# Scores of batches 4 to 7 on 64-partition heads, the first attention-values step ahead of the second scores, and the values prepared a batch ahead

## The chip, the cores and the metric

The kernel runs on one core of one Trainium2 chip. The metric is device time in microseconds (us), lower is better. The kernel before takes 320.43 us as the median of three runs (319.01 to 321.49); the profiled execution took 320.42 us, of which the span between its first and last instruction is 318.6 us.

## The reference

Two things in a row: an attention over q, k, v of shape (8 batches, 8 heads, 576 positions, 64), and a feed-forward layer over its output seen as 4608 rows of 512 columns.

```python
q_d, k_d, v_d = means of q, k, v over 4 neighbouring positions      # 144 positions
out_d = softmax(q_d @ k_d.T / 8) @ v_d                              # each row repeated 4 times
scores = where(|i - j| < 4, q @ k.T / 8, -1e9)                      # a band of 7
out   = repeat(out_d, 4) + softmax(scores) @ v
x     = out as 4608 x 512                                           # row: batch and position
h     = x @ w_in                                                    # 512 -> 2048
g     = h * sigmoid(1.702 * h)
y     = g @ w_out                                                   # 2048 -> 512
```

## The kernel before

The order of instructions on every engine is written out by hand: each engine runs its own in the order in which the program issues them, and semaphores join the engines.

**Groups.** After a prologue that does batch 0's attention, the main loop runs over nine groups `g` of 512 rows. Group `g` does the feed-forward layer of its rows: `mm1` (16 chunks of 128 hidden columns, four matmuls of 128x512 each, L712, each chunk followed by an activation `silu` on ScalarE, L723), then `mm2` (64 matmuls of 128x512, L776; after each 16 of them an output tile is scaled on ScalarE and stored from SyncE's queue). Beside that, group `g` does the attention of batch `b = g + 1`, as steps put between these matmuls. The list `POS` says where: its numbers count mm1's chunks from 0 to 15, and from 16 on mm2's matmuls (position n is matmul n - 16). The steps are, in order:

1. `s_pe(0)` at 13: the scores of heads 0 to 3 on TensorE. `scores_mixed` takes three PSUM tiles: two for the band (5 stretches of 60 queries against 64 keys, two halves `par`, four heads `r`, and two halves `a` of the head dimension: 80 matmuls of 32 rows, L360) and one for the coarse scores (24 matmuls of 32 rows and 144 columns, L372).
2. `s_act(0)` at 16: a table load, two exponentials of the band (`es`, L410) and one of the coarse scores (`ed`, L416) on ScalarE; the band mask on VectorE (`mask_local`, L424).
3. `s1` at 35: scores and exponentials of heads 4 to 7.
4. `avn(0, 1)` at 45: for head pairs 0 and 1 the products with the values, 40 matmuls each (L441 with `vb`, L463 with the coarse values `vd`), then `normalise` on VectorE (reciprocal L479, multiply L480).
5. `av_tr` at 56: the same for pairs 2 and 3, and the transposes of pair 0.
6. `tr(1, 2, 3)` at 69: the other transposes (L494, L504), copies on ScalarE (L618) and the merges into `xT` on VectorE (L639, L645). `xT` is what the next group's mm1 reads.

Three PSUM tiles `PA` of two banks go round in turn for all of these steps, two banks `PM` for the feed-forward layer.

**q and k.** A load by GpSimd's queue (`load_1`, L185) brings four heads of one batch as bf16 into 128 partitions. `prep_1` (L262) transposes 32x32 blocks on VectorE, so that head `r` lies on partitions 32r to 32r + 31, each holding pairs of head dimensions next to each other (`a`). `pool_qk` (L292, L296) sums over four positions on GpSimd, for `kdT` and `qdT`. The load buffers are double (`bufs=2`).

**Values.** SyncE's queue loads v in fp32 for the band (`vf`, ten transfers, L205, one buffer) and for the coarse sums (`v4`, six transfers, L228, one buffer). In group g GpSimd casts batch b's `vf` to `vb` (`prep_v`, L302) and sums `v4` into `vd` (`prep_v4`, L308 and L311, three times). `vbs` and `vds` are double, by the parity of the batch.

**Preparation in a group.** Before the steps, each group from 1 on issues this:

```python
if b > 2: load_v4(b)
prep_qk(b, 0); pool_qk(b, 0)
if b + 1 < B: load_qk(b + 1, 0 and 1)
prep_v(b, nc.gpsimd)
if b + 1 < B: load_v(b + 1)
prep_qk(b, 1); pool_qk(b, 1)
prep_v4(b, nc.gpsimd)
```

Of the kernel before, what the change touches and what calls it, by code (L numbers as in the profile page):

```python
# [8 lines left out]
FP32 = mybir.dt.float32  # L9
# [10 lines left out]
def kernel(  # L20
# [43 lines left out]
    eds = [persist.tile([128, 2, 480], BF16, name=f"ed{i}") for i in range(2)]  # L64
    v4 = persist.tile([128, 3, HP, 4 * D], FP32, name="v4")
    kdT = [persist.tile([128, 160, 2], BF16, name=f"kdT{i}") for i in range(NQ)]

    PA = [psum.tile([128, 2, 512], FP32, name=f"pa{i}") for i in range(3)]
    PM = [psum.tile([128, 512], FP32, name=f"pm{i}") for i in range(2)]
# [2 lines left out]
    def ps_tile(n=None):  # L72
        if n is None:
            n = turn["a"] % 3
            turn["a"] += 1
        return PA[n]
# [3 lines left out]
        return PM[turn["m"] % 2]  # L80

    wz = consts.tile([128, 512], BF16, name="wz")
    wf = consts.tile([128, 512], FP32, name="wf")
    off = consts.tile([128, 60], BF16, name="off")
    psel = consts.tile([128, 7, 64], BF16, name="psel")

# [24 lines left out]
    def fill():  # L111
        nc.vector.memset(wz, 0.0)
        nc.vector.memset(wf, 0.0)
        for t in kdT:
            nc.vector.memset(t[:, SD:160, :], 0.0)
        for t in vbs:
            nc.vector.memset(t[:, :, :, 64:65], 1.0)
        for t in vds:
            nc.vector.memset(t[:, :, :, 64:65], 4.0)
        for t in es:  # L120
            nc.vector.memset(t[:, :, 300:304], 1.0)
        for t in eds:
            nc.vector.memset(t[:, :, 432:480], 1.0)
# [56 lines left out]

    def load_1(name, src, store, b, qd):
        t = ldp.tile(
            [128, 1152], BF16, name=f"{name}b{qd}", tag=f"{name}b{qd}", bufs=2
        )
        nc.gpsimd.dma_start(  # L185
            out=t,
            in_=bass.AP(
                tensor=src.tensor, offset=src[b, 4 * qd].offset,
                ap=[[1152, 128], [1, 1152]],
            ),  # L190
        )
        store[b, qd] = t

    def load_qk(b, qd):
        load_1("k", k, kf, b, qd)
        load_1("q", q, qf, b, qd)
# [61 lines left out]
    def prep_1(name, b, qd):  # L258
        store, dst = {"k": (kf, kT), "q": (qf, qT)}[name]
        tt = work.tile([128, S, 2], BF16, name=f"{name}T{qd}", tag=f"{name}T{qd}", bufs=1)  # L260
        t32 = tt.rearrange("p t a -> p (t a)").bitcast(FP32)
        nc.vector.transpose(  # L262
            out=t32.rearrange("p (i c) -> p c i", c=18),
            in_=store[b, qd].bitcast(FP32).rearrange("p (c d) -> p c d", c=18),
        )
        dst[b, qd] = tt

    def prep_qk(b, qd):
        prep_1("k", b, qd)
        prep_1("q", b, qd)  # L270

    def new_qdT(b, qd):
        t = work.tile([128, SD, 2], BF16, name=f"qdT{qd}", tag=f"qdT{qd}", bufs=1)
# [115 lines left out]
    def scores_d(b, qd, sd):  # L389
# [3 lines left out]
                    score_d(b, qd, sd, kc, a, r)  # L393
        return sd

    def scores_mixed(b, qd):
        sp, sd = [ps_tile(), ps_tile()], ps_tile()
        for i in range(5):
            for a in range(2):
                if i >= 2:  # L400
                    for r in range(4):
                        score_d(b, qd, sd, i - 2, a, r)
                for x in (1, 0):
                    for r in range(4):
                        score(b, qd, sp, i, a, r % 2 if x == 0 else 1 - r % 2, r)
        return sp, sd
# [254 lines left out]
    def attention(b, slots=None):  # L661
        st = {}

        def s_pe(qd):
            st["s", qd], st["d", qd] = scores_mixed(b, qd)

        def s_act(qd):
            if qd == 0:
                nc.scalar.preload_act_table_set("exp_and_others")
            exp_local(qd, st["s", qd])  # L670
            exp_down(qd, st["d", qd])
            if qd == 1:
                nc.scalar.preload_act_table_set("silu_and_others")
            mask_local(qd)

        def s1():
            s_pe(1)
            s_act(1)

        def avn(*hps):  # L680
            def f():
                for hp in hps:
                    st["o", hp] = av(b, hp, slots and slots[hp % 2])
                for hp in hps:
                    st["y", hp] = normalise(st["o", hp])
            return f

        def tr(*hps):
            def f():
                for hp in hps:  # L690
                    st["x", hp] = transp(st["y", hp], slots and slots[hp % 2])
                for hp in hps:
                    od = copy_od(st["x", hp])
                    merge(b, hp, st["x", hp], od)
            return f

        first = [lambda: s_pe(0), lambda: s_act(0), s1, avn(0, 1)]
        if b == 1:
            return first + [tr(0), tr(1), avn(2, 3), tr(2), tr(3)]

        def av_tr():
            for hp in (2, 3):
                st["o", hp] = av(b, hp)
            st["x", 0] = transp(st["y", 0])
            for hp in (2, 3):
                st["y", hp] = normalise(st["o", hp])
            merge(b, 0, st["x", 0], copy_od(st["x", 0]))

        return first + [av_tr, tr(1, 2, 3)]

    def hps_mm(g, ffc, dmc, acc):
# [91 lines left out]
            f()  # L803

    POS = [13, 16, 35, 45, 56, 69]
    POS_0 = [16, 18, 30, 46, 52, 56, 65, 71, 75]
    VDP_0 = 41

# [93 lines left out]
    for g in range(n_groups):  # L902
        b = g + 1
        if g == 0:
            load_vb(1, 0)
            load_vb(1, 1)
            load_vb(1, 2)
            prep_qk(1, 0)
            pool_qk(1, 0)
            prep_qk(1, 1)  # L910
            load_vb(1, 3)
            load_vb(1, 4)
            load_w_out(2)
            load_w_out(3)
            reduce_qk(1, 1, "q")
            reduce_qk(1, 1, "k")
            for qd in range(NQ):
                load_qk(2, qd)
            nc.gpsimd.memset(v4[32:64], 0.0)
            load_v(2, gate=after(w_out_bf[0:1, 12, 0:1], nc.gpsimd))  # L920
            load_v4(2)
        elif b < B:
            if b > 2:
                load_v4(b)
            prep_qk(b, 0)
            pool_qk(b, 0)
            if b + 1 < B:
                for qd in range(NQ):
                    load_qk(b + 1, qd)
            prep_v(b, nc.gpsimd)  # L930
            if b + 1 < B:
                load_v(b + 1)
            prep_qk(b, 1)
            pool_qk(b, 1)
            prep_v4(b, nc.gpsimd)
        steps = {}
        if b < B:
            for n, f in zip(POS if g else POS_0, attention(b, None if g else (1, 2))):
                steps.setdefault(n, []).append(f)
            if g == 0:  # L940
                steps.setdefault(VDP_0, []).append(lambda: prep_vd_pe(1, flat(PA[2])))
        gT = new_gT() if g else gT0
        mm1(g, gT, steps, 0 if g else 6)
        mm2(g, gT, {n - 16: f for n, f in steps.items() if n >= 16})
# [30 lines left out]
```

## Time and profile before

| what | value |
|---|---|
| median of 3 runs | 320.43 us (319.01 to 321.49) |
| profiled execution: time, span | 320.42 us, 318.6 us |
| busy share of the span: TensorE, VectorE, ScalarE, GpSimd | 97%, 42%, 58%, 44% |
| granted TensorE clock in the 40 slices | 9 (90% or more) throughout |
| groups 3 to 6 (batches 4 to 7): length of each | 32.86, 32.99, 33.09, 32.75 us |
| group 7 (no attention): length | 27.63 us |

Times in the profile are in us from the first instruction unless marked ns. PE is TensorE's matmuls, PEld its weight loads, DVE VectorE, ACT ScalarE, POOL GpSimd, SP SyncE. A line "x32" in a timeline is 32 instructions merged, with the first one's start and the time from there to the last one's end. A 128x512 matmul is listed with 380 ns, but the next one starts 0.216 us later, so the stream is read from starts.

### The profile page before, as it was taken

Reading aid. Unit: us, or ns where it says so; the run is one execution under the profiler, and the core shown is the slowest. Engines: PE = TensorE matmul, PEld = TensorE weight load, DVE = VectorE, ACT = ScalarE, POOL = GpSimd, SP = SyncE. Lnnn points to the kernel's source line nnn. Section 1 sums busy time; section 2 is a strip of 40 time slices with the busy share of each in tenths; the row PEclk is TensorE's granted clock in tenths of the full one; section 3 lists DMA queues with packets and bytes.
Section 4 is the critical chain, followed back from the end, with each engine's and each line's share of the span. In section 5 each row is a group of like instructions: output and inputs, shape, how many; then the busy total and the mean of one; then the engine's idle time right before and its main releaser. Section 6 shows DMA issues by size and latency. Waiting matters only on the chain.

```text
span 318.6 us, 10993 instructions
## 1 busy us (share of the span) xinstructions
PE 309.5 (97%) x4927; PEld 156.9 (49%) x4927; DVE 133.6 (42%) x222; ACT 184.0 (58%) x314; POOL 138.9 (44%) x168
## 2 busy tenths in 40 slices
PE   7899999999999989999999999999999999999995
PEld 4465455444554545455545554455445544444444
DVE  6963825730684066703780378027811650000000
ACT  4464773577647674658465846674667556415611
POOL 8843782099209930696049703980297000000000
PEclk9999999999999999999999999999999999999999
DMA  7999999999719941598259915991360110020011
GB/s 121 116 191 209 184 90 207 185 270 230 180 39 218 199 114 70 144 216 173 71 134 206 188 41 136 206 205 58 109 107 2 71 68 2 0 99 33 2 65 67
DMA packets 64078, 40.02 MB, mean 126 GB/s; under 512 B 44064, under 2 KB 55456, under 8 KB 64032
## 3 DMA queue, kind: packets, MB, share of 16 engines
q0 software_dynamic: 19392, 14.95, 33.3%
q1 hardware_dynamic: 44496, 24.32, 32.7%
q8 instruction: 38, 0.62, 0.9%
q10 hardware_dynamic: 144, 0.07, 0.1%
q14 instruction: 8, 0.07, 0.1%
HBM read 44.83 MB, written 9.44 MB: 170 GB/s over the span
## 4 chain that ended last, share of the span: by engine, by line
PE 86%; DMA 7%; POOL 4%; issue 1%; ACT 0%; DVE 0%; POOLq 0%
PE pm L776 37%; PE pm L712 33%; DMA kb<-in_k_dram 5%; PE pa L360 3%; PE pa L776 2%; DMA qb<-in_q_dram 2%; PE pa L441 2%; PE pa L712 2%; PE pa L494 2%; PE pa L372 2%; PE pa L463 2%; PE pm L791 1%; POOL w_in_bf L238 1%; POOL vb L216 1%; POOL pq L292 1%
## 5 line engine op out<-in xcount | busy, mean ns | idle before, releaser
L776 PE MATMUL pm<-w_out_bf,gT 128*128 128x512 bf16 x528 | 120.8, 380 | 0.4 <-issue 0.4
L712 PE MATMUL pm<-xT,w_in_bf 128*128 128x512 bf16 x512 | 119.2, 379 | 0.0
L723 ACT ACTIVATE gT<-pm 128x512 bf16<-128x512 f32 x128 | 76.3, 598 | 44.7 <-PE pm L712 44.7
L712 PEld LDWEIGHTS <-w_in_bf 128*128 128x128 bf16 x576 | 55.6, 98 | 66.2
L776 PEld LDWEIGHTS <-gT 128*128 128x128 bf16 x560 | 52.0, 98 | 60.8 <-issue 1.7
L424 DVE TENSOR_TENSOR es<-es,mask 128x600 bf16<-128x600 bf16 x28 | 18.6, 667 | 90.1 <-ACT es L410 89.1
L292 POOL TENSOR_TENSOR pq<-kT 128x576 f32<-128x576 bf16 x13 | 15.1, 1159 | 84.7 <-DVE kT L262 84.7
L761 ACT ACTIVATE osb<-pm 128x512 f32<-128x512 f32 (+2 forms) x35 | 20.5, 586 | 38.3 <-PE pm L776 34.2
L618 ACT COPY od<-pa 128x384 f32<-128x384 f32 (+1 forms) x56 | 19.0, 406 | 26.4 <-PE pa L504 23.3
L480 DVE TENSOR_TENSOR y<-pa,rc 128x896 bf16<-128x896 f32 x28 | 30.6, 1092 | 1.0
L410 ACT ACTIVATE es<-pa 128x600 bf16<-128x600 f32 x32 | 19.7, 668 | 10.8 <-PE pa L360 10.6
L639 DVE TENSOR_TENSOR xT<-pa,od 128x570 bf16<-128x570 f32 x28 | 21.0, 752 | 8.0 <-ACT od L618 8.0
L308 POOL TENSOR_TENSOR v<-v 112x512 f32<-112x512 f32 x18 | 23.9, 1330 | 0.0
L763 DVE TENSOR_SCALAR osb<-pm 128x128 f32<-128x128 f32 x1 | 0.3, 293 | 55.0 <-ACT osb L761 55.0
L262 DVE STREAM_TRANSPOSE kT<-kb 128x576 f32<-128x576 f32 x16 | 20.0, 1248 | 5.6 <-DMA kb<-in_k_dram 5.5
L262 DVE STREAM_TRANSPOSE qT<-qb 128x576 f32<-128x576 f32 x16 | 19.8, 1240 | 0.8 <-DMA qb<-in_q_dram 0.6
L712 PE MATMUL pa<-xT,w_in_bf 128*128 128x512 bf16 x64 | 20.0, 379 | 0.0
L360 PEld LDWEIGHTS <-kT 32*64 32x64 bf16 x1280 | 14.7, 104 | 7.8 <-issue 6.6
L360 PE MATMUL pa<-qT,kT 32*64 32x60 bf16 x1280 | 17.2, 198 | 1.3 <-DVE qT L262 1.3
L216 POOL DMA_DIRECT2D vb<-in_v_dram x20 | 13.7, 699 | 8.1 <-DMA w_in_bf<-in_moe_w_in_dram 3.6
L292 POOL TENSOR_TENSOR pq<-qT 128x576 f32<-128x576 bf16 x13 | 14.9, 1147 | 0.0
L416 ACT ACTIVATE ed<-pa 128x864 bf16<-128x864 f32 x16 | 14.3, 897 | 0.1
(92 smaller groups left out, 278.9 us busy)
## 6 DMA issues: line engine op xcount, KB each, us to landing
out_dram<-osb SPq DMA_DIRECT2D x35, 256.0 KB, 2.1
vf<-in_v_dram SPq DMA_DIRECT2D x60, 128.0 KB, 5.3
v<-in_v_dram SPq DMA_DIRECT2D x36, 192.0 KB, 4.5
kb<-in_k_dram POOLq DMA_DIRECT2D x16, 288.0 KB, 6.5
qb<-in_q_dram POOLq DMA_DIRECT2D x16, 288.0 KB, 7.9
w_in_bf<-in_moe_w_in_dram POOLq DMA_DIRECT2D x4, 512.0 KB, 12.1
w_out_bf<-in_moe_w_out_dram POOLq DMA_DIRECT2D x4, 512.0 KB, 8.7
vb<-in_v_dram POOLq DMA_DIRECT2D x20, 64.0 KB, 5.7
```

The costliest lines, as they stand in the source:

```text
L262: nc.vector.transpose(out=t32.rearrange("p (i c) -> p c i", c=18), in_=store[b, qd].bitcast(FP32).rearrange("p (c d) -> p c d", c=18),)
L292: nc.gpsimd.tensor_tensor(out=t1, in0=sv[:, :, 0:2, :], in1=sv[:, :, 2:4, :], op=ALU.add)
L308: eng.tensor_tensor(out=t1[0:112], in0=x[:, :, 0:2, :], in1=x[:, :, 2:4, :], op=ALU.add)
L360: nc.tensor.matmul(sp[r // 2][64 * par : 64 * par + 64, r % 2, 60 * i : 60 * i + 60], lhsT=kT[b, qd][rows, k0 : k0 + 64, a], rhs=qT[b, qd] ...
L410: nc.scalar.activation(out=es[2 * qd + u][:, :, 0:300], in_=sp[u][:, :, 0:300], func=AF.Exp, scale=inv_sqrt_d,)
L480: nc.vector.tensor_tensor(out=y[:, xs], in0=ov[:, :, :, 0:D], in1=rc[:, xs].to_broadcast([128, n, 7, D]), op=ALU.mult,)
L618: nc.scalar.copy(out=od[:, 4 * t0 : 4 * (t0 + n)].rearrange("p (t f) -> p t f", f=4), in_=x[:, xx, 288 : 288 + n, None].to_broadcast([128, ...
L639: eng.tensor_tensor(out=sub(xT[hp], t0 + 3, (57, 2), (114, 5), (1, 57)), in0=sub(x, 3, (509, 2), (57, 5), (1, 57)), in1=sub(od, 3, (57, 2) ...
L712: nc.tensor.matmul(acc, lhsT=w_in_bf[:, dmc, ffc * 128 : (ffc + 1) * 128], rhs=xT[dmc][:, g * TG : g * TG + TG], start=(dmc == 0), stop=(d ...
L723: nc.scalar.activation(out=gT[:, ffc, :], in_=acc, func=AF.Silu, scale=GELU_SCALE)
L761: eng.activation(out=osb, in_=ap, func=AF.Copy, scale=1.0 / GELU_SCALE)
L776: nc.tensor.matmul(ops[t], lhsT=gT[:, ffc, t * 128 : (t + 1) * 128], rhs=w_out_bf[:, ffc, :], start=(ffc == 0), stop=(ffc == n_ffc - 1),)
```

## The change

For batches 4 to 7 (`WIDE = 4`, groups 3 to 6):

- After the transpose of q or k, `widen` makes a copy with a head on 64 partitions: one VectorE copy of 128 partitions x 1152 elements that separates the two halves `a`, and four copies of 32 partitions x 576 that gather each head's halves above each other. Two heads lie on the partitions at a time, the other two (`x`) behind them. `pool_wide` sums these on GpSimd as `pool_qk` did.
- `scores_wide` takes 40 matmuls of 64 rows for the band and 12 for the coarse scores, in place of 80 and 24 of 32 rows.
- The order of preparation on VectorE is: transpose k0, widen k0, transpose q0, transpose k1, widen q0, transpose q1, widen k1, widen q1. Each load for the next batch is issued behind its transpose.
- `avn(0, 1)` goes ahead of `s1`; the steps stand at `POS_W` = 14, 16, 35, 46, 59, 71.
- `vb` and `vd` of the next batch are prepared on GpSimd at the end of a group's preparation, from loads that SyncE issues at the group's start.

In all batches the load buffers of q and k are single. `wf` lies in `v4`'s memory. In groups 1 and 2 the preparation changes over: in group 1 VectorE casts `vf` and sums `v4` for batch 2, GpSimd casts batch 3's `vf`, and `v4` of batch 3 is loaded at position 70; in group 2 VectorE sums `v4` for batch 3, and GpSimd casts and sums for batch 4.

```diff
@@ persistent tiles
+    kdW = [persist.tile([128, 2, 160], BF16, name=f"kdW{i}") for i in range(NQ)]
+    qdW = [persist.tile([128, 2, SD], BF16, name=f"qdW{i}") for i in range(NQ)]
+    kW = [persist.tile([128, 2, S], BF16, name=f"kW{i}") for i in range(NQ)]
+    qW = [persist.tile([128, 2, S], BF16, name=f"qW{i}") for i in range(NQ)]
+    WIDE = 4
-    wf = consts.tile([128, 512], FP32, name="wf")
+    wf = v4.rearrange("p k h c -> p (k h c)")[:, 0:512]
@@ fill()
+        for t in kdW:
+            nc.vector.memset(t[:, :, SD:160], 0.0)
@@ load_1()
-            [128, 1152], BF16, name=f"{name}b{qd}", tag=f"{name}b{qd}", bufs=2
+            [128, 1152], BF16, name=f"{name}b{qd}", tag=f"{name}b{qd}", bufs=1
@@ new functions
+    def widen(name, b, qd):
+        src = (kT if name == "k" else qT)[b, qd]
+        w = (kW if name == "k" else qW)[qd]
+        nc.vector.tensor_copy(out=w, in_=src.rearrange("p t a -> p a t"))
+        for s in range(2):
+            lo, hi = slice(64 * s, 64 * s + 32), slice(64 * s + 32, 64 * s + 64)
+            nc.vector.tensor_copy(out=w[hi, 0, :], in_=w[lo, 1, :])
+            nc.vector.tensor_copy(out=w[lo, 1, :], in_=src[hi, :, 0])
+
+    def pool_wide(name, qd):
+        src, dst = (kW[qd], kdW[qd][:, :, 0:SD]) if name == "k" else (qW[qd], qdW[qd])
+        sv = src.rearrange("p x (j f) -> p (x j) f", f=4)
+        t1 = work.tile([128, 2, SD, 2], FP32, name="pq", tag="pq")
+        nc.gpsimd.tensor_tensor(
+            out=t1.rearrange("p x j f -> p (x j) f"),
+            in0=sv[:, :, 0:2], in1=sv[:, :, 2:4], op=ALU.add,
+        )
+        nc.gpsimd.tensor_tensor(
+            out=dst, in0=t1[:, :, :, 0], in1=t1[:, :, :, 1], op=ALU.add
+        )
+
+    def prep_wide(b):
+        def turn_load(name, qd):
+            prep_1(name, b, qd)
+            if b + 1 < B:
+                load_1(name, *((k, kf) if name == "k" else (q, qf)), b + 1, qd)
+        def finish(name, qd):
+            widen(name, b, qd)
+            pool_wide(name, qd)
+        turn_load("k", 0)
+        finish("k", 0)
+        turn_load("q", 0)
+        turn_load("k", 1)
+        finish("q", 0)
+        turn_load("q", 1)
+        finish("k", 1)
+        finish("q", 1)
+
+    def scores_wide(qd):
+        sp, sd = [ps_tile(), ps_tile()], ps_tile()
+        for i in range(5):
+            for x in range(2):
+                for s in range(2):
+                    rows = slice(64 * s, 64 * s + 64)
+                    for par in range(2):
+                        k0 = 114 * i + KSTART[par]
+                        q0 = 114 * i + QSTART[par]
+                        nc.tensor.matmul(
+                            sp[s][64 * par : 64 * par + 64, x, 60 * i : 60 * i + 60],
+                            lhsT=kW[qd][rows, x, k0 : k0 + 64],
+                            rhs=qW[qd][rows, x, q0 : q0 + 60],
+                            start=True, stop=True,
+                            tile_position=(64 * s, 64 * par),
+                        )
+            if 1 <= i < 4:
+                kc = i - 1
+                for s in range(2):
+                    rows = slice(64 * s, 64 * s + 64)
+                    for x in range(2):
+                        nc.tensor.matmul(
+                            sd[64 * x : 64 * x + 64, s, SD * kc : SD * kc + SD],
+                            lhsT=kdW[qd][rows, x, 48 * kc : 48 * kc + 64],
+                            rhs=qdW[qd][rows, x, :],
+                            start=True, stop=True,
+                            tile_position=(64 * s, 64 * x),
+                        )
+        return sp, sd
@@ scores_mixed()
+        if b >= WIDE:
+            return scores_wide(qd)
@@ attention()
+        if b >= WIDE:
+            first = first[:2] + [avn(0, 1), s1]
@@ main loop
     POS = [13, 16, 35, 45, 56, 69]
+    POS_W = [14, 16, 35, 46, 59, 71]
...
-        elif b < B:
-            if b > 2:
-                load_v4(b)
+        elif b < WIDE:
+            if b == WIDE - 1:
+                load_v(b + 1)
             prep_qk(b, 0)
             pool_qk(b, 0)
-            if b + 1 < B:
-                for qd in range(NQ):
-                    load_qk(b + 1, qd)
-            prep_v(b, nc.gpsimd)
+            prep_qk(b, 1)
+            for qd in range(NQ):
+                load_qk(b + 1, qd)
+            if b < WIDE - 1:
+                prep_v(b, nc.vector)
+                load_v(b + 1)
+            prep_v4(b, nc.vector)
+            pool_qk(b, 1)
+            prep_v(b + 1, nc.gpsimd)
+            if b == WIDE - 1:
+                load_v4(b + 1)
+                prep_v4(b + 1, nc.gpsimd)
+        elif b < B:
             if b + 1 < B:
                 load_v(b + 1)
-            prep_qk(b, 1)
-            pool_qk(b, 1)
-            prep_v4(b, nc.gpsimd)
+                load_v4(b + 1)
+            prep_wide(b)
+            if b + 1 < B:
+                prep_v(b + 1, nc.gpsimd)
+                prep_v4(b + 1, nc.gpsimd)
         steps = {}
         if b < B:
-            for n, f in zip(POS if g else POS_0, attention(b, None if g else (1, 2))):
+            for n, f in zip(POS_W if b >= WIDE else POS if g else POS_0, attention(b, None if g else (1, 2))):
                 steps.setdefault(n, []).append(f)
+            if b == WIDE - 2:
+                steps.setdefault(70, []).append(lambda: load_v4(WIDE - 1))
```

## The prediction

> **What bounds the kernel now.** I read the page first (busy shares, chain that ended last), then the windows view over groups 3 to 7, then timelines of single groups. TensorE is busy 97% of the span and makes 86% of the chain; no other engine reaches 60%.
>
> ```profile
> PE 309.5 (97%) x4927; PEld 156.9 (49%) x4927; DVE 133.6 (42%) x222; ACT 184.0 (58%) x314; POOL 138.9 (44%) x168
> ...
> PE 86%; DMA 7%; POOL 4%; issue 1%; ACT 0%; DVE 0%; POOLq 0%
> ```
>
> So what counts is each stretch in which TensorE's stream is not a 128x512 matmul. In the windows view, columns are length, then busy time per engine:
>
> ```profile
> 128.40:161.26 32.86, 32.86 (x601) 16.59 (x600) 15.90 (x25) 21.02 (x36) 17.75 (x19) 1.00 0.67 147
> 161.26:194.25 32.99, 32.99 (x601) 16.68 (x600) 15.93 (x25) 21.03 (x36) 17.76 (x19) 1.00 0.70 146
> 194.25:227.34 33.09, 33.09 (x601) 16.78 (x600) 15.89 (x25) 21.02 (x36) 17.76 (x19) 1.00 0.71 145
> 227.34:260.09 32.75, 32.75 (x602) 16.50 (x600) 14.95 (x25) 21.02 (x36) 15.24 (x15) 1.00 0.30 70
> 260.09:287.72 27.63, 27.63 (x130) 12.54 (x128) 0.64 (x2) 11.83 (x20) 0.00 (x0) 1.00 0.10 39
> ```
>
> Groups 3 to 6 take 131.69 us; group 7, with no attention, takes 27.63, which is 128 matmuls at 0.2158. Attention costs TensorE 5.1 to 5.5 us a group, VectorE 16 of 33 us, GpSimd 18. What a burst costs is read from its neighbours' starts:
>
> ```profile
> 242.30 4.05 PE L776 MATMUL pm<-w_out_bf,gT 128*128 128x512 bf16 x18
> 246.28 0.33 PE L360 MATMUL pa<-qT,kT 32*64 32x60 bf16 x32
> ...
> 247.26 2.33 PE L776 MATMUL pm<-w_out_bf,gT 128*128 128x512 bf16 x10
> 249.53 0.35 PE L441 MATMUL pa<-vb,es 64*64 64x65 bf16 x20
> ...
> 250.34 0.82 PE L776 MATMUL pm<-w_out_bf,gT 128*128 128x512 bf16 x3
> ```
>
> The last of the 18 starts at 242.30 + 4.05 - 0.38 = 245.97, the next is due at 246.19 and comes at 247.26: the 104 score matmuls cost 1.08. The same for the values: due 249.43, comes 250.34: 80 matmuls of 64x64 tiles cost 0.91. Each burst has 0.09 before its first small matmul and 0.12 after the start of its last, so 0.21 of edges: 8.4 ns for each 32-row matmul, 8.75 ns for each 64-row one.
>
> **The sum. First term, TensorE.** The eight score bursts of groups 3 to 6 cost 1.19, 1.08, 1.18, 1.22, 1.20, 1.08, 1.08, 1.08: 9.11 us. After, each has 52 matmuls of 64 rows. At the value row's 8.75 ns that is 0.21 + 0.455 = 0.665. Twelve of them stream 144 columns over four tiles, which no 64-row row here does; at double price they add 0.105: 0.77. I take 0.70. Eight give 5.6: a gain of 3.5 us (bounds 2.95 and 3.8). Moving `avn(0, 1)` forward moves 0.91 and removes nothing.
>
> **Second term, what VectorE must finish in time.** Twenty copies a group are added to VectorE, ahead of its masks. No such copy stands in the trace. Rows near it:
>
> ```profile
> L262 DVE STREAM_TRANSPOSE kT<-kb 128x576 f32<-128x576 f32 x16 | 20.0, 1248 | 5.6 <-DMA kb<-in_k_dram 5.5
> L281 DVE TENSOR_REDUCE kdT<-kT 128x288 bf16<-128x1152 bf16 x3 | 4.0, 1325 | 0.0
> ```
>
> ```profile
> 211.93 1.96 DVE L424 TENSOR_TENSOR es<-es,mask 128x600 bf16<-128x600 bf16 x2 [12.60 <-ACT es L410]
> 215.14 1.03 DVE L424 TENSOR_TENSOR es<-es,mask 128x600 bf16<-128x600 bf16 x2 [1.26 <-ACT es L410]
> ...
> 212.06 1.49 POOL L308 TENSOR_TENSOR v<-v 112x512 f32<-112x512 f32 x1
> ```
>
> The first fence is from the groups by form (busy, then mean ns), the second from a timeline of group 5. One mask alone takes 0.47 for 600 bf16 elements; the smallest VectorE instructions (six elements, L645) take 0.17. So the fast rate is 0.17 plus 0.5 ns an element; the slow rate, from the reduction, is about 0.1 plus 1.08 ns an element. Fast, the 1152 copy is 0.76 and the strided 576 copies 0.46 each; the two dense ones I put halfway between 0.17 and 0.46, 0.31, since a copy reads one tensor and the mask two. With 0.03 between dependent instructions a widening is 2.45. Slow, it is 1.33 + 4 x 0.72 + 0.15 = 4.35; an absolute floor is five times 0.17, 0.85. I take 2.45: bf16 elementwise in SBUF is the mask's kind, not the reduction's.
>
> Now one wide group, time 0 at its first matmul. In group 5 the last merge ended 0.8 after the next group's start; `tr` moves two matmuls later, so VectorE is free at 1.26. Transpose and widening of k0 end at 4.96, transposes q0 and k1 at 7.3, widening q0 at 9.75; GpSimd's two sums (1.15 + 0.67, rows L292 and L296) give `qdW` at 11.7. `s_pe(0)` is due after 56 matmuls, 12.1: 0.4 to spare. Then transpose q1 and two widenings end at 15.9. The first exponential is ready 2.78 after mm2's start (group 5: 209.11 and 211.89), at 17.3, the second 0.56 later; `avn(0, 1)` is due at 14.5 + 19 x 0.2158 = 18.6. So it fits by about 0.8 if nothing is held up.
>
> But the pair of masks at 211.93 took 1.96 and not 1.03, under GpSimd's L308 which itself took 1.49 and not 1.27: VectorE's two-input instruction waits out a running GpSimd sum, and the reverse. If copies wait as masks do, the sums of q0, k1 and q1 fall between them: up to 0.6 in widening k1, up to 1.6 in widening q1, and 0.9 more between the first two masks. That makes the prep end at 17.5 to 18 and the second mask at 19.4 to 19.9, against a need at about 19.05 for pair 1: a stall of 0.4 to 0.9. If copies don't wait, none. I take 0.25 a group, near the lower end of 0 to 0.9, since transposes under GpSimd's sums show no stretch (1.24 to 1.26 throughout) and only part of the queue can be held: 1.0 us for four groups.
>
> [...]
>
> **What costs nothing, and under which cover.** `s1` now needs the two PSUM tiles that `normalise` of pairs 0 and 1 frees: in group 6 its second multiply ended 2.4 after the burst (252.75 against 250.34), and `s1` is due 2.37 + 0.09 behind it and writes that tile last, so it fits by about 0.1; whatever delays the masks delays both alike. The four loads of a wide group (0.56 each on GpSimd's queue) go out while GpSimd waits for copies. Single load buffers: the loads for batch 1 now wait for batch 0's transposes, which end at 12.4, before the queue reaches them (16.36); in wide groups each load follows its transpose and has 20 us to land, against a median of 6.5 to 7.9. Group 1: VectorE casts 2560 elements (2.8 at the slow rate) and does three pairs of sums (0.7 + 0.4); `vf` lands about 67.8, `v4` about 70.1 (last issue plus 5.3 and 4.5), so it ends near 74, and VectorE's first mask is at 78.97. Group 2: `v4` is issued at position 70, lands near 98, three sums end near 102, first mask at 111.98. SyncE's queue has 16 value loads ahead of the stores: they wait only on preparation that ended in the group before, 11.5 of issue against 20 us to the first store. GpSimd's cast and sums for the next batch run to about 27 of 32 and have half a group to spare. Two memsets more in the prologue fall in 1.1 us of VectorE's idle time; `wf` in `v4` delays nothing, since its reader ends by 26 and `v4`'s memset is at 47. If the cover of group 1 failed, its masks would be late: 1 to 2 us, once.
>
> The sum is made against the profiled 320.42 (span 318.6 and 1.8 around it), the same as the median of 320.43: 320.42 - 3.5 + 1.0 = 317.9.
>
> **Rivals.**
> - *No stall.* Copies don't wait for GpSimd, or the prep ends by 17 anyway. 320.42 - 3.8 = 316.6, to 316.9. For: 0.8 to spare. Against: the masks' row.
> - *GpSimd in between* (the other side). Prep ends behind 18.6, from which on each us late is a us of TensorE's idle time ahead of `avn(0, 1)`, with `s_pe(0)` late as well since the 0.4 to spare goes first. At 1.6 a group: 320.42 - 3.5 + 6.4 = 323.3; it decides from 0.9 a group. For: 25.7 of 32 us of VectorE busy, and three GpSimd pairs in its way. Against: only two of four widenings meet them.
> - *Copies at one element a cycle.* Widening 4.35: q0 ends at 13.5, its sums at 15.4 (3.1 late), all prep at 23.5, another 2.3 late: 5.4 x 4 - 3.5 = 338.5. For: the reduction. Against: the mask.
> - *No gain on TensorE.* 32-row tiles are eight at once and 64-row ones four; if a tile's time and not the issue limits, 52 cost what 104 did: 320.42 + 0.3 = 320.7. Against: the value bursts use four tiles at 8.75 ns. [...]
>
> **How the numbers follow.** A change of 1% (3.2 us) is about what a measurement of this kernel tells from none, since its runs spread over 2.5 us. Chances: forecast (317.0 to 319.0) 0.43, of which 0.15 below 317.2; no stall 0.20; no gain 0.07; GpSimd in between 0.20 (319 to 326, about a third of it within 1%); slow copies 0.10. Faster by over 1%: 0.20 + 0.15 = 0.35. Slower by over 1%: 0.13 + 0.10 = 0.23. Within: 0.42. The range runs from 316.2 to 325.0, leaving out the slow copies and the ends of the others, about 0.17; the forecast's own range is 317.0 to 319.0.
>
> **What would show it.** Right: score bursts of groups 3 to 6 at 0.67 to 0.77; copies of 0.76, 0.46 and 0.31; the last copy of a group at 16 to 18 after its start; an idle TensorE of 0.1 to 0.5 ahead of the first values; groups of 32.1 to 32.4. Wrong: bursts over 0.9, a first copy near 1.3, masks that wait for copies by over 1 us, or stalls in groups 1 and 2.

## The result, and the profile after

The changed kernel takes 323.12 us as the median of 20 runs (320.64 to 327.45), the kernel before 320.39 (319.01 to 322.57); the ratio is 1.0059 (95% interval 1.0039 to 1.008). So it is slower by 0.6%, where 317.9 us and faster was predicted. Ratios here leave out executions more than 1.5% above the fastest of their kernel, medians do not. The profiled execution took 322.66 us, its span is 320.9 (before: 318.6).

The page of the changed kernel, busy time and chain:

```profile
PE 305.4 (95%) x4511; PEld 153.2 (48%) x4511; DVE 194.7 (61%) x317; ACT 183.7 (57%) x314; POOL 132.9 (41%) x155
...
PE 87%; DMA 3%; issue 3%; DVE 2%; ACT 2%; POOL 2%; POOLq 0%
```

TensorE is now busy for 4 us less than before, in a span that is 2.3 longer: it stands still for 6 us more. The chain has 3% of "issue", time in which an engine waited for nothing that the profile names. The windows of groups 3 to 6 say where (length, then busy time per engine):

```profile
130.20:164.58 34.38, 32.30 (x498) 15.95 (x497) 27.26 (x43) 20.76 (x36) 18.83 (x19) 1.00 0.72 140
164.58:197.17 32.59, 32.28 (x498) 15.86 (x497) 28.21 (x45) 20.95 (x38) 19.26 (x19) 1.00 0.76 147
197.17:229.76 32.59, 32.28 (x497) 15.87 (x496) 28.39 (x45) 20.94 (x38) 19.29 (x19) 1.00 0.76 147
229.76:262.17 32.41, 32.24 (x497) 15.87 (x496) 26.62 (x45) 20.95 (x38) 8.35 (x8) 1.00 0.09 35
```

Groups 4 to 6 became shorter (before 32.99, 33.09, 32.75), group 3 longer by 1.5 us, with 2.1 us of it idle. In each of them TensorE works some 32.3. Group lengths, from the first matmul of mm1 to that of the next group, with the kernels run later ("start" is the prologue):

| kernel | start | g0 | g1 | g2 | g3 | g4 | g5 | g6 |
|---|---|---|---|---|---|---|---|---|
| before | 23.80 | 37.45 | 32.93 | 34.05 | 32.86 | 32.99 | 33.09 | 32.75 |
| after | 24.49 | 37.32 | 34.01 | 34.39 | 34.38 | 32.59 | 32.60 | 32.41 |
| after, values loaded once | 23.80 | 35.93 | 32.76 | 33.11 | 32.11 | 32.59 | 32.58 | 32.39 |
| before, values loaded once | 22.97 | 37.26 | 32.75 | 32.99 | 32.75 | 32.76 | 32.94 | 32.75 |
| values alone | 24.08 | 36.71 | 32.90 | 37.21 | 32.89 | 34.11 | 34.47 | 32.76 |
| coarse values late | 23.52 | 36.74 | 33.17 | 33.97 | 33.66 | 32.59 | 32.59 | 32.40 |
| loads early | 23.58 | 36.59 | 32.98 | 35.40 | 32.22 | 32.48 | 32.65 | 32.39 |
| early, and late once | 23.49 | 37.53 | 32.92 | 32.97 | 36.68 | 32.53 | 32.64 | 32.40 |

Up to the end of group 0 the changed kernel and its five variants here run the same program, yet their prologues take 23.49 to 24.49 and their groups 0 take 35.93 to 37.53. Differences of that size in these two columns come from the single execution and not from an edit.

Where TensorE stands still, from the timeline of group 3 around `s1` and from the list of waits (waiter, releaser, total, times, longest):

```profile
152.71 0.24 PE L464 MATMUL pa<-qdW,kdW 64*64 64x144 bf16 x4
155.02 0.25 PE L452 MATMUL pa<-qW,kW 64*64 64x60 bf16 x8 [2.08 <-issue]
155.21 2.98 PE L857 MATMUL pm<-w_out_bf,gT 128*128 128x512 bf16 x13
```

```profile
PE pa L520 <- issue: 2.4, 2, 1.4
...
PE pa L452 <- issue: 2.1, 1, 2.1
...
PE pm L857 <- issue: 1.2, 1, 1.2
```

TensorE stops in the middle of a burst, between two scores whose operands, `kW` and `qW`, the matmuls before them have already read. No engine is named. Group 1 has such a stop in `av_tr` (2.25 where 1.13 is normal), group 2 in `avn(0, 1)` (2.54 where 0.91 is normal; before had one there too, 2.05), group 3 in `s1` (2.99 where 0.72 is).

**What it waits for.** The page counts 35 packets on a queue of the kind "instruction" with 0.57 MB, 16 KB each. TensorE executes 4511 matmuls and 4511 weight loads, some 258 to a packet; before it was 9854 and 38 packets, 259 to each. I read them as TensorE's instructions, brought in blocks of some 256, an estimate from these counts. Two answers for the DMA queues, the first for 147.1 to 152.4 us, the second the instruction queue's line for 152.4 to 153.8 (packets, MB, share of 16 engines):

```profile
q1 hardware_dynamic: 1068, 1.05, 114.6%
```

```profile
q8 instruction: 1, 0.02, 5.6%
```

For 5.3 us SyncE's transfers fill the DMA engines (114.6%) and no block moves; then one does, it lands at 153.71, and TensorE goes on at 155.02. To place the blocks, TensorE's instructions are counted from 0, matmuls and weight loads together, and the blocks from 0 too. In the traces with few transfers, block n mostly begins 1 to 2 us after instruction 256n + 157; I call the start of that instruction "asked". In the seven traces that hold every matmul, TensorE never started instruction 256n + 449 less than 1.2 us after block n had landed. In the same traces, 43 blocks from number 8 on were asked when the mean DMA share of the next 4 us was over 1.0 (packets overlap in time, so the share can pass 1): they began a median 3.8 us after the asking (2.3 to 6.4). For 93 blocks asked at a share under 0.2 the median was 1.3 us. A matmul of 128x512 with its weight load takes 0.2158 us, so the 292 instructions between the two are some 31 us of cover; inside the bursts 80 matmuls with their loads pass in 0.91 us. So I take it that a block that begins 3 us later than usual can be missed there, as block 18 was (5.35 us behind the asking, a stop of 2.08).

| block | kernel | asked | began | landed | TensorE at 256n + 449 |
|---|---|---|---|---|---|
| 14 (group 2) | before | 113.49 | 115.08 | 116.75 | 118.24, after a stop |
| 14 | after | 115.03 | 117.42 | 118.68 | 120.28, after a stop |
| 18 (group 3) | before | 140.27 | 143.50 | 144.84 | 148.14, no stop |
| 18 | after | 147.12 | 152.47 | 153.71 | 155.03, after a stop |
| 18 | loads early | 145.47 | 147.85 | 149.09 | 151.12, no stop |

The last row is counted by weight loads alone, two instructions for each, since that trace lacks 50 of the 4511 matmuls.

The transfers themselves, from the timelines of SyncE's queue in group 3 (before, then after; `v` is `v4`):

```profile
129.49 4.69 SPq L228 DMA_DIRECT2D v<-in_v_dram  x6
138.52 8.79 SPq L205 DMA_DIRECT2D vf<-in_v_dram  x10
```

```profile
131.45 11.65 SPq L212 DMA_DIRECT2D vf<-in_v_dram  x10
143.21 3.27 SPq L235 DMA_DIRECT2D v<-in_v_dram  x6
```

The bytes are the same. Before, they come in two parts with a pause of 4.3 us; after, in one piece, which began in this group 1.3 us after its start and kept the DMA engines full to 152.

### The profile page after: what moved, and what is told of

The parts are those of the page before. It is cut to its first block, busy times and chain, and to the rows that moved or that the text cites. A ratio compares the mean times of both kernels' runs of the same rounds, so it can differ in the third digit from the quotient of the medians.

```text
span 320.9 us, 10270 instructions
## 1 busy us (share of the span) xinstructions
PE 305.4 (95%) x4511; PEld 153.2 (48%) x4511; DVE 194.7 (61%) x317; ACT 183.7 (57%) x314; POOL 132.9 (41%) x155
## 4 chain that ended last, share of the span: by engine, by line
PE 87%; DMA 3%; issue 3%; DVE 2%; ACT 2%; POOL 2%; POOLq 0%
PE pm L793 35%; PE pm L857 33%; PE pa L793 4%; DMA vb<-in_v_dram 3%; PE pa L857 2%; PE pa L520 2%; DVE es L503 2%; PE pa L573 2%; PE pa L542 1%; ACT L748 1%; PE pa L452 1%; PE pm L872 1%; PE pa L407 1%; ACT es L489 1%; PE pa L419 1%
## 5 line engine op out<-in xcount | busy, mean ns | idle before, releaser
L503 DVE TENSOR_TENSOR es<-es,mask 128x600 bf16<-128x600 bf16 x28 | 24.2, 888 | 35.2 <-ACT es L489 34.7
L349 POOL CAST vb<-vf 128x2560 bf16<-128x2560 f32 x5 | 12.1, 2428 | 19.5 <-DMA vf<-in_v_dram 19.4
L192 POOL DMA_DIRECT2D kb<-in_k_dram x16 | 9.3, 582 | 25.4 <-DVE kT L269 24.1
L292 POOL TENSOR_TENSOR pq<-kW 128x576 f32<-128x576 bf16 x8 | 11.4, 1425 | 19.0 <-DVE kW L286 19.0
L355 POOL TENSOR_TENSOR v<-v 112x512 f32<-112x512 f32 x12 | 15.8, 1320 | 0.1
L339 POOL TENSOR_TENSOR pq<-kT 128x576 f32<-128x576 bf16 x5 | 6.4, 1288 | 21.4 <-DVE kT L269 21.3
```

Source lines behind the costliest of these rows:

```text
L355: eng.tensor_tensor(out=t1[0:112], in0=x[:, :, 0:2, :], in1=x[:, :, 2:4, :], op=ALU.add)
L503: nc.vector.tensor_tensor(out=ev, in0=ev, in1=mask, op=ALU.mult)
```

## The experiments

**Values loaded once.** The changed kernel without the loads of the values of batches 3 to 7, which use batch 2's.

```diff
     def load_v(b, gate=None, chunks=range(5)):
+        if b > 2:
+            vf[b] = vf[2]
+            return
...
     def load_v4(b):
+        if b > 2:
+            return
```

> The changed kernel with the values of batches 3 to 7 not loaded: the casts and sums run as before, on batch 2's values, so some 5 x 16 transfers on SyncE's queue are left out. In the profile of the changed kernel three bursts are long with the chain naming 'issue' (TensorE waits for no semaphore): 2.25 instead of 1.13 in group 1, 2.54 instead of 0.91 in group 2, 2.99 instead of 0.72 in group 3, 5.0 us together; each one falls where TensorE's 256-instruction block (16 KB, queue q8) began to arrive late while the transfers were dense. Theory A (late instruction blocks behind dense transfers): with the transfers thinned out the blocks come in time, the three bursts fall to 1.2, 1.0 and 0.8, groups 1 to 3 lose 3 to 5 us, time 318.5 to 320. Theory B (the time is lost to VectorE and GpSimd holding each other up ahead of the masks, the transfers don't matter): the three bursts stay long, time 322 to 323.

Measured: 316.84 us (315.76 to 317.41), ratio to the kernel before 0.989 (0.9844 to 0.9936). The long bursts of groups 1 to 3 are gone, groups 4 to 6 are unchanged to 0.02 us. So the loss is where the values' transfers are. Groups 1 to 3 together are 4.8 us shorter, close to the 5.0 that the three bursts had over their normal length. The prologue and group 0 are 2.1 shorter as well, but nothing that the edit leaves out lies there; that part comes from the single execution. The time is below the 318.5 that was expected at the least.

**The control: before, values loaded once.** The same edit in the kernel before.

> The kernel before, with the values of batches 3 to 7 not loaded: those batches use the values of batch 2. It is the control to the same edit of the changed kernel, which took 316.84. Theory A: the kernel before had late instruction blocks too, but fewer (a burst of 2.05 in group 2 where 0.91 is normal, group 0 at 37.45 against 35.93), so it gains 1 to 3 us: 317.5 to 319.4, still above 316.84 by what the wide scores bring. Rival C (what the values' transfers cost is the same for both kernels, so that they do not explain a difference): it gains as much as the changed kernel did, 6 us: 314 to 315. Rival D (no cost before): 320.4.

Measured: 318.36 us (316.68 to 319.5), ratio 0.9925 (0.9897 to 0.9953). The kernel before pays for the transfers too, some 0.75% or 2.4 us; the changed one pays 1.0059 against 0.989, 1.7% or 5.4 us. By the intervals each cost is known to within 1 to 2 us. Groups 3 to 6 without the transfers are 131.20 before and 129.67 after: what the wide scores bring, net of their own stalls, is 1.5 us.

**All TensorE instructions 42 later, after and before.** The 21 matmuls of 336 columns that `warm` puts in the prologue become 42 of 168, so that every later instruction stands 42 places further in its block.

```diff
-    warm(21, 336)
+    warm(42, 168)
```

> The changed kernel with 42 warm-up matmuls of 168 columns in place of 21 of 336 at the start, so that all of TensorE's later instructions move by 42 places against the 256-instruction blocks; nothing else moves. Theory A: the blocks that were late in groups 1, 2 and 3 are asked for 2 to 4.5 us earlier, the three long bursts fall to about 1.2, 1.0 and 0.8, time 318 to 319.5. Theory B: no change, 322.5 to 323.5, the same bursts long.

> The kernel before with the same 42 warm-up matmuls. Theory A: its one long burst (2.05 instead of 0.91, first values of group 2) falls to 0.9 to 1.0; time 319 to 320, unless another block now becomes late (then 320 to 322). Theory B: within 0.2% of the kernel before.

Measured: after 322.13 us (319.82 to 325.76), ratio 1.0035 (1.0 to 1.007); before 321.85 (319.83 to 329.4), ratio 1.0048 (1.0016 to 1.0079). The shift did not cure the changed kernel, for which theory A had expected 318 to 319.5: the stops of groups 1 and 3 vanished, the one of group 2 grew to 3.3 us, group 5 got one of 1.2. It did cost the kernel before as much as the change had cost. I read this as the place of the instructions in their blocks deciding which late block is missed; a difference of 0.5% between two versions of this kernel can be that alone.

**Coarse sums of the heads once.** The changed kernel with GpSimd's sums for `kdW` and `qdW` left out for batches 5 to 7, which use batch 4's.

```diff
             widen(name, b, qd)
-            pool_wide(name, qd)
+            if b == WIDE:
+                pool_wide(name, qd)
```

> The changed kernel with GpSimd's coarse sums of q and k left out for batches 5 to 7 (the scores use batch 4's). Theory B (VectorE's copies and masks wait out GpSimd's sums, and the first values wait for the masks): the first values' burst of groups 4 to 6 falls from 1.45, 1.46 and 1.27 to 0.9 to 1.0, 1.3 us together, and the copies of widening q1 fall from 0.85 to 1.13 to 0.30 to 0.45. Theory A says the same of these bursts, but that the loss of 5.0 us in groups 1 to 3 stays: time 321.5 to 322. Under theory B alone the time would come to 319 or less.

Measured: 321.63 us (320.17 to 325.12), ratio 1.0038 (1.0004 to 1.0071). Groups 4 and 6 take 32.05 where they took 32.59 and 32.41: the stop ahead of the first values is gone with the sums. Group 5 has one all the same (32.98): GpSimd's cast of 2.32 us, which waited for its transfer, fell on the first mask there, which took 2.22 in place of 0.47. Groups 1 to 3 kept their stops, and that of group 2 grew to 3.3 us.

**Values alone.** Loads and preparation of the values as in the changed kernel, scores of all batches as before.

```diff
-            prep_wide(b)
+            prep_qk(b, 0); pool_qk(b, 0); prep_qk(b, 1)
+            # loads of batch b + 1, as before
+            pool_qk(b, 1)
...
-        if b >= WIDE:
-            return scores_wide(qd)
```

> The changed kernel's handling of the values, loads and the changeover in groups 1 and 2, but the scores of all batches on 32 partitions in the order of before, with no VectorE copies. Theory A: the loss of about 5 us comes with the values' transfers, so that this half alone is slower than before by 2 to 5 us: 322.5 to 325.5. Rival E (the loss comes with the widening and the moved first values): not slower than before, 319.5 to 321.

Measured: 325.94 us (323.41 to 327.27), ratio 1.0159 (1.0118 to 1.0199). The values' half of the change costs 1.6%, and the wide scores, added to it, give 1% back. Here the stops are in the first values of groups 2, 4 and 5 (4.12, 2.26 and 2.55 where 0.91 is normal).

**Wide scores alone.** The other half: values as before, a batch prepared in its own group.

```diff
...
+            load_v4(b)
+            turn_load(b, "k", 0); finish(b, "k", 0)
+            prep_v(b, nc.gpsimd)                      # and load_v(b + 1)
+            turn_load(b, "q", 0); turn_load(b, "k", 1); finish(b, "q", 0)
+            turn_load(b, "q", 1)
+            prep_v4(b, nc.gpsimd)
+            finish(b, "k", 1); finish(b, "q", 1)
```

> Wide scores with their VectorE copies and the first values ahead of the second scores, as in the changed kernel, but with the values as in the kernel before (a batch prepared in its own group, on GpSimd, loads at the places of before); in the wide groups GpSimd casts the values behind the first key's sums and sums the coarse values ahead of the second heads' sums. Theory A: without the changed transfers the widening keeps most of its gain of 3.5 us on TensorE, less some stall at the first and second values: 317.5 to 319.5, groups 4 to 6 at 32.2 to 32.8. Rival E (the widening and the moved values are the loss): 321 or more.

Measured: 352.41 us (350.76 to 352.87), ratio 1.099 (1.0961 to 1.1019), groups 3 to 6 at 40.7 to 41.1. Theory A missed this; rival E's "321 or more" holds, but nothing in it foresaw 10%. Two lines of the timelines of GpSimd and VectorE in group 5 show why:

```profile
215.37 2.32 POOL L339 CAST vb<-vf 128x2560 bf16<-128x2560 f32 x1
```

```profile
215.67 2.64 DVE L282 COPY qW<-qT 128x1152 bf16<-128x1152 bf16 x1
```

A copy that takes 0.76 elsewhere waited out the cast. Copies beside the coarse values' sums took up to 2.0 us, the first mask started 24.0 us after its group's start (17.4 in the changed kernel), and TensorE stood 4 us ahead of the first values. After each of these stops the granted clock was half for 6.8 us. So the halves cannot be taken apart in this way: with the values a batch ahead, GpSimd's 8 to 9 us of casts and sums come behind VectorE's copies, and here they fall among them. Whether another order of the same work would do without the move was not tried.

**Coarse values late.** In groups 2 to 6 the six coarse loads and their sums move behind the first store.

```diff
-                load_v4(b + 1)                        # at the start of the group
+                steps[36]: load_v4(b + 1); prep_v4(b + 1, nc.gpsimd)
```

> The changed kernel, with the loads of the coarse values (six transfers) and their sums moved from the start of groups 2 to 6 to position 36 of mm2, where SyncE's queue holds them behind the first store, so that the ten loads of the local values have the start of the group to themselves. Theory A (TensorE waits for its own instruction blocks, which come late when SyncE's transfers are dense): the dense stretch of a group is halved, the long bursts of groups 2 and 3 (2.54 and 2.99 us) shrink to under 1.5, and the time is 319.5 to 321.5 against 323.1. Rival B (the loss is the position of TensorE's instructions against the blocks, or the changeover's own work in groups 1 to 3): the bursts stay long or others take their place, 322.5 to 324. Both: the stall ahead of the first values in groups 4 to 6 stays at about 0.5 us.

Measured: 321.25 us (319.17 to 322.93), ratio 1.0029 (1.0004 to 1.0053). As theory A has it, the two long bursts are gone (1.21 and 0.72), but as the rival has it, others of 2.04 and 1.58 have come, where the coarse loads now are.

**Coarse values late, attention steps later.** The same, with `POS_W` from 35, 46, 59, 71 to 37, 48, 61, 72.

> The changed kernel with the coarse values' loads and sums at position 36 of mm2 in groups 2 to 6, and the first values, second scores, second values and transposes of the wide groups two positions later (one for the transposes). If both theory A and the reading of the stall ahead of the first values (VectorE's masks late behind GpSimd's sums, 0.4 to 0.55 us in groups 4 to 6) hold: 0.4 us a group less than the variant with late coarse values alone, 318 to 320. If the masks' lateness only moves on to the second values: no difference from that variant.

Measured: 325.08 us (322.19 to 328.24), ratio 1.011 (1.0067 to 1.0152): a miss. The first values no longer wait for masks (0.91 to 1.03), yet the transposes at 72 got stops of 0.2 to 0.7, and groups 4 to 6 gained nothing (32.56, 32.93, 32.44). The rest I read as late blocks again, with stops of 1.7 us in group 2 and 3.2 in group 3, where no engine is named: with the steps moved, others were missed.

**Loads early.** The loads of both kinds of values for batch 4 on go out at position 74 of the group before, behind its third store.

```diff
-                load_v(b + 1)                         # at the start of the group
-                load_v4(b + 1)
...
+            if WIDE - 1 <= b < B - 2:
+                steps[74]: load_v(b + 2); load_v4(b + 2)
```

> The changed kernel, with the loads of both kinds of values of batches 4 and later issued at position 74 of mm2 of the group before, behind its third store, instead of at the start of the group: some 3 us earlier, so that the dense stretch (4 to 22 us after a group's start in group 3) ends before most of the small matmuls. Theory A (instruction blocks late behind dense transfers, waited for where small matmuls use up 256 instructions in few us): the long bursts of groups 2 and 3 shrink to under 1.5 and the time is 318.5 to 321 against 323.1. Rival B (it is the position of TensorE's instructions against the blocks, whatever the transfers do): 322 to 324.5. Both: 0.4 to 0.5 us ahead of the first values of groups 4 to 6 stay.

Measured: 318.94 us (317.79 to 321.33), ratio 0.9957 (0.9935 to 0.9979): faster than the kernel before by 0.4% and than the changed one by 1%, with the same work as the changed one. The windows of group 3 between 16 and 24 us after its start (after, then loads early; the last two columns are DMA share and GB/s):

```profile
146.00:150.00 4.00, 4.00 (x95) 2.13 (x94) 3.04 (x7) 3.35 (x5) 2.83 (x3) 1.00 1.14 194
150.00:154.00 4.00, 2.94 (x55) 1.40 (x54) 2.13 (x3) 0.00 (x0) 3.92 (x4) 1.00 0.85 171
```

```profile
144.50:148.50 4.00, 3.84 (x95) 2.12 (x94) 3.07 (x6) 3.20 (x5) 3.08 (x3) 1.00 0.29 61
148.50:152.50 4.00, 3.84 (x67) 1.98 (x68) 2.36 (x4) 1.07 (x2) 3.92 (x4) 1.00 0.19 70
```

At the same place of the program the DMA engines are quiet and TensorE works through (the 0.16 us short of 4.00 in each line are matmuls that this trace lacks). Group 3 is 2.2 us shorter. Group 2 still has a stop of 2.6; the coarse loads of batch 4 stayed in its middle.

**Early, and late once.** That load moved to position 65 of group 2.

> The variant with early loads, and in group 2 the coarse values of batch 4 loaded and summed from position 65 of mm2, behind the third store, instead of in the middle of the group (issued 107.5 to 112.5, where TensorE then waited 2.6 us in the first values). Theory A: group 2 falls from 35.40 to 33 or 33.5, group 3 loses at most 1 us to GpSimd's sums at its start, and the time is 316.5 to 318.5 against 318.94. Rival B: group 2 keeps a stall of 2 us and more somewhere, and the time is 318.5 to 320.

Measured: 321.68 us (321.23 to 324.03), ratio 1.0039 (1.0005 to 1.0073), above both ranges. Group 2 fell to 32.97, as theory A says, but group 3 rose to 36.68, since GpSimd now sums batch 4's coarse values at its start, beside the first widening: TensorE waited 2.1 us for `qdW` in its first scores, and right after its scores its granted clock was half for 3.4 us (on such stretches see the last section).

**More transfers in the kernel before.** Twelve transfers of 96 KB that nobody reads.

```diff
             load_v(b + 1)
+            if b > 2:
+                load_more(b + 1)
```

> The kernel before with twelve more transfers (96 KB each, into a tile that nobody reads) on SyncE's queue behind the local values' loads of groups 2 to 6, so that the dense stretch of a group ends some 6 us later; no engine waits for them but SyncE's own stores behind them. Theory A: TensorE's blocks come late in the bursts at 19 to 30 us of a group, with bursts of 2 us and more for TensorE waiting on nothing that the profile names, 2 to 8 us in all: 322.5 to 328. Rival (TensorE's idle time comes from VectorE or GpSimd, or the late blocks from something else than transfers): 320 to 321. The same would come if stores held back TensorE's PSUM tiles: then the idle time would stand ahead of mm2's matmuls, with ScalarE as the releaser.

Measured: 326.35 us (322.95 to 329.45), ratio 1.0162 (1.0123 to 1.02). Waits of its profiled execution:

```profile
PE pa L453 <- issue: 2.8, 2, 1.9
...
PE pa L475 <- POOL vd L323: 4.2, 3, 2.0
```

The time lies in theory A's range, but the trace bears it out in part only. Of the two stops without a name, that of 1.9 us in group 4 is new; that of 0.9 in group 2 the kernel before has too. The longest stops are in group 5, where the coarse values came late (the second line), which I had not foreseen, and the granted clock was half for 6.8 us behind the first of them. So the 6 us are at least two effects. The traced execution was also the slowest of the six (329.45 us; the others took 322.95 to 326.46). This run does not prove theory A.

## Why the prediction was wrong, by its own steps

**First term, right.** The forecast was 320.42 - 3.5 + 1.0. Seven of the eight score bursts take 0.72 (0.70 was put, and the long one without its stop is another 0.72), so TensorE's attention fell by 9.11 - 5.76 = 3.35 us. A little of it was luck in the yardstick: without the transfers all bursts of before take 1.08, 8.64 in all, so the wide scores as such are worth 2.9.

**Second term, right in kind, low in size.** This is the 1.0 of that sum. The copies take 0.76, 0.30 and 0.45, as read from the masks' row; the rival of slow copies, 1.33 and 0.72, is out. Under GpSimd's sums they stretch (timelines of group 4, VectorE, then GpSimd, then TensorE):

```profile
175.27 0.74 DVE L282 COPY kW<-kT 128x1152 bf16<-128x1152 bf16 x1
...
178.93 1.13 DVE L285 COPY qW<-qW 32x576 bf16<-32x576 bf16 x1
180.09 0.85 DVE L286 COPY qW<-qT 32x576 bf16<-32x576 bf16 x1
...
181.95 2.21 DVE L503 TENSOR_TENSOR es<-es,mask 128x600 bf16<-128x600 bf16 x2 [0.19 <-ACT es L489]
```

```profile
178.19 1.71 POOL L292 TENSOR_TENSOR pq<-kW 128x576 f32<-128x576 bf16 x1 [1.15 <-DVE kW L286]
```

```profile
184.22 0.35 PE L520 MATMUL pa<-vb,es 64*64 64x65 bf16 x20 [0.31 <-DVE es L503]
```

The copy of 1.13 (0.30 when alone) waited for the sum of 1.71 (1.14 when alone). The last copy ends 17.2 us after the group's start, inside the 16 to 18 that was forecast, but the two masks take 2.21 together, and the second pair of values waits. The stops of groups 3 to 6 are 0.07, 0.54, 0.55 and 0.36: 1.5 us, where 0.25 a group had been put. That is 0.4 us a group, not the 0.9 that the prediction worked out as the end.

**What costs nothing: the step that failed.** The prediction let SyncE's sixteen loads ahead of the stores cost nothing, since the stores had time and the values had half a group to land, and gave groups 1 and 2 a cover of their own. It asked for each transfer whether its reader would wait. It did not ask what else rides on the DMA engines. The runs point to TensorE's own instructions there (35 packets of the kind "instruction", 16 KB each): with the values loaded once the changed kernel takes 316.84, and with the same loads moved out of the bursts 318.94. Against the span: score bursts -3.35, first values +1.5, the stop in `s1` of group 3 +2.27, group 1 +1.08, group 2 +0.34, prologue and group 0 +0.56 (+0.69 and -0.13), 2.4 in all, against the measured 2.3. So the term that was put at nothing came to 3.7 us in this trace; the 0.56 is no bigger than the spread of these two stretches between executions. The named sign, "stalls in groups 1 and 2", came true, though not by its mechanism: VectorE's masks were in time there (the long stops name no engine), and what came late was, as I read it, TensorE's own instructions.

The row was there to be read before. Its burst of 2.05 in group 2 was such a stop, and four of the eight score bursts at 1.18 to 1.22 stood over the 1.08 of the rest; both were taken as they were, with no question what made them long.

**The rivals.** None of them was it. "GpSimd in between" gives the right time, 323.3, by the wrong cause: the stall was 0.4 a group and not 1.6. That the whole range, 316.2 to 325.0, takes in the measured time is owed to this rival, and is luck. "No stall" is out by the stops of 0.36 to 0.55 in groups 4 to 6. "No gain on TensorE" is out by the bursts.

**What stays open.** That the packets are TensorE's instructions is inferred from their count, and at which instruction a block is asked for from when blocks begin in quiet stretches; no record shows the request. And 0.5% of this comparison can be the chance of which block meets which transfer, as the shift showed for the kernel before, so the 0.6% between the two kernels as they stand is not itself proof of anything; that the values' transfers as placed by the change cost more than those before rests on the larger differences, 1.0159 for that half alone and 0.989 without them.

## What to carry to other kernels

In this kernel what I read as TensorE's program came as DMA packets beside the data's, and in the densest stretches (a DMA share over 1.0) began a median 3.8 us after the asking, where a burst of 80 small matmuls took 0.91: where bursts of small matmuls lie, keep large transfers out, or let them end before (318.94 here against 323.12). When a bulk load is moved, look at what the DMA share is over the time of the bursts before and after, and not only at whether the reader gets its data in time. A burst that is longer than its twins in the profile before, with "issue" as the releaser, is a price that the next change can raise (2.05 here against 0.91, and 2.54 after), and a shift of some instructions tells how much of a small difference is such chance (0.5% here).

## What the runs showed of the hardware

On a queue of the kind "instruction" 35 packets of 16 KB came, one for some 258 of TensorE's instructions. In the seven traces that were counted they began a median 3.8 us after what is called the asking above when the DMA share was over 1.0, 1.3 us at under 0.2, and TensorE started instruction 256n + 449 at the earliest 1.2 us after block n had landed.

A stop of TensorE cost more than itself in some of these runs. In the variant with values alone, TensorE stood from 116.7 to 119.5, 2.81 us; in the windows after it (PEclk is the third column from the end) the granted clock was half:

```profile
119.00:120.00 1.00, 0.47 (x22) 0.45 (x22) 0.89 (x1) 0.00 (x0) 1.00 (x2) 0.61 0.02 8
120.00:121.00 1.00, 1.00 (x9) 0.40 (x4) 0.80 (x2) 0.00 (x0) 0.92 (x2) 0.50 0.06 16
121.00:122.00 1.00, 1.00 (x4) 0.34 (x3) 0.54 (x1) 0.45 (x1) 1.00 (x2) 0.50 0.00 0
122.00:123.00 1.00, 1.00 (x4) 0.37 (x3) 0.00 (x0) 0.15 (x1) 0.92 (x2) 0.68 0.00 0
```

A mean of 0.61 is 0.78 us at half, one of 0.68 is 0.64, so the stretch is 3.4 us long. Matmuls of 128x512 start 0.43 us apart in it instead of 0.2158, which added 1.2 us to the stop.

In the early, and late once variant the windows from 143 to 147, after the stop of 2.12 us for `qdW`, have 0.60, 0.50, 0.50 and 0.70, so 3.4 us at half as well. Where wide scores stood alone (mean clock 0.960), and with more transfers (0.990), it was 6.8 us; by their mean clocks of 0.995, 0.995 and 0.984 the traced executions of sums once and of the shifted kernels after and before held some 3, 3 and 10 us at half. In the 3.4 us ahead of the stretch TensorE had been busy for 0.9 us with values alone and for 1.3 in early, and late once. With the later attention steps a stop of 3.04 us cost nothing more: the granted clock stayed at 1.00 in all windows from 152 to 164, though TensorE was busy for 1.08 us of the 4 from 156 to 160. What decides behind which stop the clock falls, these runs do not show.

The clock record of the traced execution of the changed kernel holds no such stretch, but by their mean clocks others held some: 3.4 us at half in 321 us lower the mean to 0.995, and 12 of its 20 executions stand at 0.995 or less (322.45 to 327.45 us). Its eight others have a median of 322.27, against 320.39 for the kernel before. Of the 81 executions of the kernel before that were run beside the experiments, 7 stand at 0.995 or less. So part of the loss in the median goes with such stretches, which the one trace does not show.

A VectorE copy with one input was held up beside a GpSimd instruction as a mask with two was: in wide scores alone the copy took 2.64 us instead of 0.76 beside a cast of 2.32, in the kernel before a mask in group 5 took 1.39 instead of 0.47 beside a sum of 1.49.
